# Dealing 384 weight rows over the DMA engines by another table

## Chip, cores and metric

The kernel runs on one core of a Trainium2 chip. The metric is the device time of one execution in microseconds, as the median of several executions. "Before" is the kernel given, "the changed kernel" is the one with the diff below. All verdicts use runs in the fast state; on this one core a slow run shows by its time alone: the 78.30 us run of before beside e1 has a granted clock of 0.835, where the fast runs of that job have 0.805 to 0.841. Ratios are the mean time of one kernel's fast runs over that of the other's in the same rounds, so they are not quite the ratio of the medians quoted beside them.

## The reference

One decode step of attention over a cached window, gated by a small MLP. Only the shapes matter here (shortened, not the full source):

```python
def reference(A_x, A_k_cache, A_v_cache, A_wq, A_wo, B_x, B_w1, B_b1, B_w2, B_b2):
    x = A_x                                   # (4, 1, 512), bf16
    xn = _layernorm(x)
    q = xn @ wq                               # wq 512 x 4096: 32 heads of 128
    k, v = last 1024 positions of the caches  # 8 kv heads, batch 4: 1 MB each a head
    o = softmax(q k^T * 128**-0.5) v
    s = o.reshape(4, 1, 4096) @ wo            # wo 4096 x 512: 4 MB
    g = silu(mlp(layernorm(xn)))              # w1 512 x 1792, w2 1792 x 512
    return x + s * g
```

Everything is read once, 28.85 MB. The time is nearly that of this stream: the DMA engines are 90% busy or more in 35 of 40 slices (below).

## The kernel before

The large loads are issued by SyncE (SP) in one long queue: wq, four K tiles, w1, the other four K tiles, four V tiles, w2, the other four V tiles, and then wo. The order of the last ones is what matters:

```python
    for n, (g0, g1) in enumerate(((0, 2), (2, 4), (4, 6), (6, 7))):
        load_wo(n, g0, g1, 0, 4)              # 1 MB, 1 MB, 1 MB, 0.5 MB
    d_w1st = pg.dma("sp", "w1st", lambda e: e.dma_start(
        wo_sb[:, 7, 0, :], A_wo[7 * 512:7 * 512 + 128, :]))      # 128 KB
```

The remaining 384 rows of wo (1 KB each) belong to the last head group. GpSimd loads them, in twelve calls, in the middle of the kernel:

```python
    R1 = (7 * 512 + 128) * D
    XS, b0 = [], 0
    for p0, n, r in ((0, 3, 5), (12, 2, 3), (20, 3, 1), (64, 2, 1), (72, 4, 5), (88, 2, 1)):
        XS.append((p0, n, r, b0))
        b0 += 4 * n * r
    XS = [(p0 + 32 * h, n, r, b + 192 * h) for h in range(2) for p0, n, r, b in XS]
    d_wox = [pg.dma("gp", "wox%d" % p0, lambda e, p0=p0, n=n, r=r, b=b: e.dma_start(
        wox_sb[p0:p0 + 4 * n, 0:r, :].rearrange("p j o -> p (j o)"),
        bass.AP(A_wo.tensor, R1 + b * D, [[r * D, n], [n * r * D, 4], [1, r * D]])), t_q)
        for p0, n, r, b in XS]
```

A call (p0, n, r) puts r rows into each of 4n partitions from p0 on. The first dimension of its source is n, and the table means it to run on the next n DMA engines, so that the six calls of a half take each of the 16 once. The packets of before fit this: q0 has 56 of 5120 bytes, 8 of 6144 and 14 of 4096, on 7 engines (3 + 4), 2 and 7 (3 + 2 + 2). The engine numbers below are names in this order; the label runs e1 and e2 test them. Each engine thus gets 4 partitions in each of the two halves: one row a partition is 8 KB an engine over both. The table is a hand-made dealing: engines 0 to 2 get 5 rows a partition, 3 and 4 get 3, 5 to 9 get 1, 10 to 13 get 5, and 14 and 15 get 1.

Because the rows then lie scattered over the partitions, GpSimd also builds 0/1 selector matrices, with which PE brings the attention output into the same order before it multiplies by the weights:

```python
    def rows_last():
        def fn(pe):
            for a in range(5):
                for j in range(3):
                    last = pe.matmul(psx[:, 160 + a * 4:164 + a * 4], selx[:, j, a, :],
                                     OTb[:, o + 4 + 4 * j:o + 8 + 4 * j], ...)
    ...
            wo([(wox_sb[:, a, :], OWx[:, a * 4:(a + 1) * 4], False, False) for a in range(5)],
               row_x, *d_wox)
```

The softmax here doesn't subtract the row's maximum and nothing guards it: scores larger than these inputs give would overflow.

Of the kernel before, what the change touches and what calls it, by code (L numbers as in the profile page):

```python
# [19 lines left out]
class _Program:  # L20
# [22 lines left out]
    def add(self, eng, fn, *deps, cls=None):  # L43
        op = _Op(eng, fn, deps, cls=cls)
        if eng == "pe":
            op.seg, op.once = self.seg, self.once
            if self.seg not in self.segs:
                self.segs.append(self.seg)
        self.ops[eng].append(op)
        return op  # L50
# [111 lines left out]
def bass_recurrent_scan__sliding_block_cached__mixer_channel_mlp__decode_kernel(  # L162
# [17 lines left out]
    BF16 = dt.bfloat16  # L180
    F32 = dt.float32

    B, D = 4, 512
# [22 lines left out]
    sb = nc.alloc_sbuf_tensor  # L206
# [4 lines left out]
    wq_sb = sb([128, 4, HQ * DH], BF16)  # L211
# [1 line left out]
    w1_sb = sb([128, 4, F], BF16)  # L213
    w2_sb = sb([128, FC, D], BF16)

    wox_sb = wq_sb[:, 0, 0:5 * D].rearrange("p (j o) -> p j o", j=5)
    kt_buf = sb([128, NKT, UT * 128], BF16)
    P_buf = sb([128, HKV, NC * 16], BF16)

# [33 lines left out]
    b2_sb = sb([4, 128], BF16)  # L253
    sel = sb([128, 4, 32], BF16)
    OW = sb([128, 4, 28], BF16)
    selx = sb([128, 3, 5, 128], BF16)
    OWx = sb([128, 20], BF16)
    hT = sb([128, FC, 32], BF16)

    OTb = sb([128, HKV * 16], BF16)  # L260
# [17 lines left out]
    add = pg.add  # L278
# [71 lines left out]
    a = add("act", lambda e: e.activation(sq1[:, :], vt1[:, :], AF.Sqrt), v)  # L350
# [9 lines left out]
    a = add("act", lambda e: e.activation(sq2[:, :], vt2[:, :], AF.Sqrt), v)  # L360
# [239 lines left out]

    R1 = (7 * 512 + 128) * D
    XS, b0 = [], 0
    for p0, n, r in ((0, 3, 5), (12, 2, 3), (20, 3, 1), (64, 2, 1), (72, 4, 5), (88, 2, 1)):
        XS.append((p0, n, r, b0))
        b0 += 4 * n * r
    XS = [(p0 + 32 * h, n, r, b + 192 * h) for h in range(2) for p0, n, r, b in XS]
# [13 lines left out]
    psx = psS[0]  # L620
# [16 lines left out]
    def rows_last():  # L637
        def fn(pe):
            last = None
            o = 7 * 16  # L640
            for a in range(5):
                for j in range(3):
                    last = pe.matmul(psx[:, 160 + a * 4:164 + a * 4], selx[:, j, a, :],
                                     OTb[:, o + 4 + 4 * j:o + 8 + 4 * j],
                                     start=(j == 0), stop=(j == 2))
            return last
        t = add("pe", fn, ep[HKV - 1], c_sx)
        return add("dve", lambda e: e.tensor_copy(OWx[:, :], psx[:, 160:180]), t)

    for g in range(HKV):  # L650
        pg.seg = ("v", g // NG)
# [31 lines left out]
    def wo(tiles, *deps):  # L683

        def fn(pe):
            last = None
            for w, o, st, sp in tiles:
                for c in range(4):
                    last = pe.matmul(psM[:, PS_W + c * 4:PS_W + (c + 1) * 4],  # L689
                                     w[:, c * 128:(c + 1) * 128], o,  # L690
                                     start=(st and c == 0), stop=sp, skip_group_check=True)
            return last
        return add("pe", fn, *deps)

    for g0, g1, i0, i1, d in d_wo:
        wo([(wo_sb[:, g, i, :], OW[:, i, g * 4:(g + 1) * 4], g == 0 and i == 0, False)
            for g in range(g0, g1) for i in range(i0, i1)], d, row_w, mlp["g"])
        if g0 == 0:
            row_x = rows_last()
            wo([(wox_sb[:, a, :], OWx[:, a * 4:(a + 1) * 4], False, False) for a in range(5)],  # L700
               row_x, *d_wox)
    t_w = wo([(wo_sb[:, 7, 0, :], OTb[:, 7 * 16:7 * 16 + 4], False, True)], d_w1st,
             ep[HKV - 1])
# [6 lines left out]
    t = add("pe", lambda pe: pe.transpose(psS[0][0:16, 0:128], sg_sb[:, :], ident32[:, :]),  # L710
            v, c_id32)
# [56 lines left out]
```

## Time and profile before

| what | value | from |
|---|---|---|
| time | 77.11 us (76.94 to 77.13, 3 runs) | timed runs |
| span of the profiled run | 75.0 us | page |
| DMA | 28.95 MB, mean 386 GB/s, 90% busy or more in 35 of 40 slices | page |
| busiest compute engine | PE, 67% of the span | page |
| end of the chain | fourth wo load lands at 71.52 us, then a tail | chain |

The way to read it: when the DMA line is full almost from end to end and every compute engine has room, look for what ends the transfers. In before's trace each wo load has 16 landing events; those of the fourth come between 69.77 and 71.52 us, and PE goes on at 71.57, after the last. So the balance between the engines counts (e4 tests it), and the page shows only their mean. Below, a "heavy" engine is one that gets 5 or 6 rows a partition from the table, and a "light" one gets 1.

### The profile page before, as it was taken

What the parts mean: (1) busy time and instruction counts of PE and PEld (TensorE: products, weight loads), DVE (VectorE), ACT (ScalarE), POOL (GpSimd) and SP (SyncE); (2) the same over time, 40 slices, a digit from 0 to 9 for tenths busy, and PEclk for the clock granted to TensorE, in tenths of its full rate; (3) what the DMA queues carried; (4) which work ended last, traced back from release to release, by engine and by line L of the source; (5) the groups of instructions that cost most, each with busy time, mean ns of one, the idle gap of its engine ahead of it and who ended that gap; (6) DMA issues with size and microseconds to landing.
All of it is one profiled execution on the core that took longest, in us unless ns stands there. A gap on an engine that the chain in (4) does not pass through costs nothing.

```text
span 75.0 us, 2371 instructions
## 1 busy us (share of the span) xinstructions
PE 50.3 (67%) x1043; PEld 40.5 (54%) x1043; DVE 40.6 (54%) x84; ACT 12.5 (17%) x21; POOL 17.8 (24%) x46
## 2 busy tenths in 40 slices
PE   0000650959999997297999959880669984686560
PEld 0000300259999996387999837650329753486430
DVE  0778200036999986097999904999800576430020
ACT  0611000090002304100311333841030000000000
POOL 6994000089999872000000000000000000000000
PEclk9999999999999999999999999995555555555555
DMA  1899999999999999999999999999999999999800
GB/s 28 262 419 422 456 419 411 428 424 428 414 456 429 410 395 422 410 425 428 428 424 428 419 424 457 435 420 400 424 428 419 428 421 408 424 419 419 314 4 2
DMA packets 4680, 28.95 MB, mean 386 GB/s; under 512 B 1007, under 2 KB 1139, under 8 KB 2114
## 3 DMA queue, kind: packets, MB, share of 16 engines
q1 hardware_dynamic: 4016, 28.45, 91.0%
q0 software_dynamic: 608, 0.40, 1.7%
q8 instruction: 5, 0.08, 0.4%
q10 hardware_dynamic: 50, 0.01, 0.1%
q14 instruction: 1, 0.01, 0.0%
HBM read 28.85 MB, written 0.00 MB: 384 GB/s over the span
## 4 chain that ended last, share of the span: by engine, by line
DMA 26%; PE 19%; DVE 3%; SPq 2%; ACT 2%; issue 1%
DMA wo_sb<-in_A_wo_dram 26%; PE psK L383 8%; PE psS L403 4%; PE psO L422 3%; SPq L674 2%; PE psK L514 1%; PE psM L689 1%; PE psS L399 1%; DVE kt_buf L524 1%; DVE den_sb L439 1%; ACT P_buf L411 1%; ACT kt_buf L523 1%; PE psS L429 1%; PE psS L710 1%; PE psK L518 0%
## 5 line engine op out<-in xcount | busy, mean ns | idle before, releaser
L389 DVE COPY kt_buf<-psK 128x1024 bf16<-128x1024 bf16 x32 | 20.9, 690 | 4.2 <-PE psK L383 4.2
L383 PE MATMUL psK<-ident,kv_buf 128*128 128x128 bf16 x256 | 19.9, 228 | 2.2 <-PEq L101 2.2
L383 PEld LDWEIGHTS psK<-ident,kv_buf 128*128 128x128 bf16 x256 | 16.0, 103 | 2.4 <-issue 1.8
L403 PE MATMUL psS<-qR,kt_buf 128*128 128x16 bf16 x256 | 10.5, 170 | 0.0
L403 PEld LDWEIGHTS psS<-qR,kt_buf 128*128 128x128 bf16 x256 | 9.6, 96 | 1.1
L422 PEld LDWEIGHTS psO<-P_buf,kv_buf 128*128 128x128 bf16 x256 | 7.5, 101 | 3.7 <-issue 2.0
L422 PE MATMUL psO<-P_buf,kv_buf 128*128 128x16 bf16 x256 | 7.9, 172 | 1.6 <-PEq L101 1.3
L607 POOL DMA_DIRECT2D wq_sb<-in_A_wo_dram x12 | 6.7, 604 | 8.5 <-PE psO L471 8.5
L411 ACT ACTIVATE P_buf<-psS 128x512 bf16<-128x512 f32 x8 | 4.8, 597 | 22.4 <-PE psS L403 22.4
L439 DVE TENSOR_REDUCE den_sb<-psS 128x16 f32<-128x512 f32 x8 | 5.5, 682 | 1.3 <-PE psS L429 1.2
L471 PE MATMUL psO<-wq_sb,xT 128*32 128x512 bf16 x32 | 3.8, 627 | 3.0 <-DMA wq_sb<-in_A_wq_dram 2.7
L455 PE MATMUL psS<-ident,xn_bf 4*128 4x4 bf16 x4 | 0.3, 172 | 7.8 <-DVE y_bf L362 7.8
L689 PE MATMUL psM<-OW,wo_sb 128*128 128x4 bf16 x112 | 3.6, 167 | 2.3 <-DMA wo_sb<-in_A_wo_dram 2.3
L689 PEld LDWEIGHTS psM<-OW,wo_sb 128*128 128x128 bf16 x112 | 3.3, 104 | 2.6 <-DMA wo_sb<-in_A_wo_dram 2.5
L455 PEld LDWEIGHTS psS<-ident,xn_bf 4*128 4x128 bf16 x4 | 0.2, 114 | 7.8 <-DVE y_bf L362 7.8
L477 DVE CAST q_sb<-psO 128x512 bf16<-128x512 f32 x1 | 0.7, 691 | 6.6 <-PE psO L471 6.6
L615 POOL TENSOR_SCALAR_AFFINE_SELECT selx<-ones_bf 128x8 bf16<-128x8 bf16 (+4 forms) x14 | 4.0, 282 | 1.0
L429 PE MATMUL psS<-P_buf,ones_bf 128*128 128x512 bf16 x8 | 3.9, 482 | 0.0
L548 PE MATMUL psK<-w_sb,hT 128*4 128x512 bf16 (+1 forms) x14 | 1.9, 622 | 2.9 <-DMA w_sb<-in_B_w_dram 2.9
L471 PEld LDWEIGHTS psO<-wq_sb,xT 128*32 128x32 bf16 x32 | 0.9, 128 | 5.1 <-DMA wq_sb<-in_A_wq_dram 3.7
L399 PE MATMUL psS<-negm,ind 128*128 128x512 bf16 x8 | 3.0, 379 | 0.0
L706 DVE TENSOR_TENSOR sg_sb<-psM,g_sb 128x16 f32<-128x16 f32 x1 | 0.2, 184 | 5.2 <-PE psM L689 5.2
(80 smaller groups left out, 43.7 us busy)
## 6 DMA issues: line engine op xcount, KB each, us to landing
kv_buf<-in_A_k_cache_dram SPq DMA_DIRECT2D x8, 1024.0 KB, 12.5
kv_buf<-in_A_v_cache_dram SPq DMA_DIRECT2D x8, 1024.0 KB, 12.4
wq_sb<-in_A_wq_dram SPq DMA_DIRECT2D x2, 2048.0 KB, 9.6
w_sb<-in_B_w_dram SPq DMA_DIRECT2D x2, 1792.0 KB, 22.5
wo_sb<-in_A_wo_dram SPq DMA_DIRECT2D x3, 1024.0 KB, 16.5
wo_sb<-in_A_wo_dram SPq DMA_DIRECT2D x1, 512.0 KB, 19.2
wq_sb<-in_A_wo_dram POOLq DMA_DIRECT2D x2, 80.0 KB, 11.9
wo_sb<-in_A_wo_dram SPq DMA_DIRECT2D x1, 128.0 KB, 17.5
```

The source lines that it names most:

```text
L383: last = pe.transpose(psK[n % NB][:, j * 128:(j + 1) * 128], kv_buf[:, lg, u * UT + j, :], ident[:, :])
L389: cp[r, n] = bank[n % NB] = add("dve", lambda e: e.tensor_copy(kt_buf[:, n % NKT, :], psK[n % NB][:, 0:1024]), t, kt_user[n % NKT], cls="cp")
L399: pe.matmul(psS[lg % 2][:, 0:512], ind[:, :], negm[:, :], start=True, stop=False, skip_group_check=True)
L403: last = pe.matmul(psS[lg % 2][:, c * 16:(c + 1) * 16], kt_buf[:, n % NKT, j * 128:(j + 1) * 128], qR[:, lg * 16:(lg + 1) * 16], start=Fal ...
L411: ex[g] = add("act", lambda e: e.activation(P_buf[:, g, :], psS[lg % 2][:, 0:512], AF.Exp, scale=SCALE), sc[r, n], cls="ex")
L422: last = pe.matmul(pso[:, 0:16], kv_buf[:, NG + lg, c, :], P_buf[:, lg, c * 16:(c + 1) * 16], start=(c == 0), stop=(c == NC - 1))
L429: den[g] = add("pe", lambda pe: pe.matmul(psS[g % 2][:, 0:512], ones_bf[:, :], P_buf[:, lg, :], start=True, stop=True))
L439: v = add("dve", lambda e: e.tensor_reduce(den_sb[:, cs], bass.AP(psS[g % 2], 0, [[512, 128], [1, 16], [16, NC]]), AX.X, ALU.add), den[g])
L471: last = pe.matmul(psO[m // 4][32 * s:32 * s + 32, 0:512], xT[:, c, :], wq_sb[:, c, m * 512:(m + 1) * 512], start=(c == 0), stop=(c == 3), ...
L607: d_wox = [pg.dma("gp", "wox%d" % p0, lambda e, p0=p0, n=n, r=r, b=b: e.dma_start(wox_sb[p0:p0 + 4 * n, 0:r, :].rearrange("p j o -> p (j o)"),
L615: c_sx = add("gp", lambda e, p0=p0, n=n, r=r, b=b, j=j: e.affine_select(selx[:, j, 0:r, p0:p0 + 4 * n], ones_bf[:, 0:4 * n * r], [[1, r], ...
L689: last = pe.matmul(psM[:, PS_W + c * 4:PS_W + (c + 1) * 4], w[:, c * 128:(c + 1) * 128], o, start=(st and c == 0), stop=sp, skip_group_che ...
```

## The change

The intent is to move rows from engines that finish late to engines that finish early. Engines 0 to 2 and 11 to 13 get 6 rows a partition instead of 5, engines 3 and 4 get 2 instead of 3, and engine 10 gets 1 instead of 5. The total stays at 384 rows in twelve calls. Six row slots in place of five make PE's part a little longer.

```diff
-    wox_sb = wq_sb[:, 0, 0:5 * D].rearrange("p (j o) -> p j o", j=5)
+    wox_sb = wq_sb[:, 0, 0:6 * D].rearrange("p (j o) -> p j o", j=6)
...
-    selx = sb([128, 3, 5, 128], BF16)
-    OWx = sb([128, 20], BF16)
+    selx = sb([128, 3, 6, 128], BF16)
+    OWx = sb([128, 24], BF16)
...
-    for p0, n, r in ((0, 3, 5), (12, 2, 3), (20, 3, 1), (64, 2, 1), (72, 4, 5), (88, 2, 1)):
+    for p0, n, r in ((0, 3, 6), (12, 2, 2), (20, 3, 1), (64, 3, 1), (76, 3, 6), (88, 2, 1)):
...
-            for a in range(5):
+            for a in range(6):
...
-        return add("dve", lambda e: e.tensor_copy(OWx[:, :], psx[:, 160:180]), t)
+        return add("dve", lambda e: e.tensor_copy(OWx[:, :], psx[:, 160:184]), t)
...
-            wo([(wox_sb[:, a, :], OWx[:, a * 4:(a + 1) * 4], False, False) for a in range(5)],
+            wo([(wox_sb[:, a, :], OWx[:, a * 4:(a + 1) * 4], False, False) for a in range(6)],
```

## The prediction

What the first rival would cost, and its chance of one in six, which moved the point to 77.05 and the range up to 77.45, were estimates; measured are the two parts of the delay, 0.9 us for a fetch and 0.5 us on the packet behind it. That a load waits for its last engine is shown by the 16 landing events above.

> **What bounds the kernel now.** I read four views, in this order: the page's slices and queues, the chain that ended last, the busy time by stretch near the end, and the timeline of the same stretch. The page first:

> ```profile
> DMA  1899999999999999999999999999999999999800
> ...
> q1 hardware_dynamic: 4016, 28.45, 91.0%
> q0 software_dynamic: 608, 0.40, 1.7%
> q8 instruction: 5, 0.08, 0.4%
> ...
> q14 instruction: 1, 0.01, 0.0%
> ```

> The DMA engines are full from slice 2 to slice 37 of 40, so the 28.95 MB stream sets the length and no compute engine does. The twelve GpSimd loads are q0: 0.40 MB, 1.7% of the engines' time. They load rows 128 to 511 of the last head's output weights, 384 rows of 1 KB, dealt unevenly over the DMA engines. The chain confirms which load ends it:

> ```profile
> 52.35 19.17 DMA wo_sb<-in_A_wo_dram
> 71.52 0.05 issue
> 71.57 0.70 PE psM L689 x20
> ...
> 72.30 0.20 DVE sg_sb L706
> ...
> 72.54 0.40 PE psS L710
> ...
> 72.96 0.28 DVE o_bf L712
> ```

> Here the fourth output-weight load lands at 71.52, and a fixed tail follows: 20 matmuls, a multiply, a transpose, an add and the store. A load has landed only when its slowest DMA engine is done, so what counts is the last engine, not the mean. The stretches (length, then busy time and count of each engine, then granted clock, DMA share, GB/s) show that the engines don't end together:

> ```profile
> 63.00:69.70 6.70, 4.88 (x148) 4.10 (x148) 1.82 (x7) 0.00 (x0) 0.00 (x0) 0.50 1.02 420
> 69.70:70.30 0.60, 0.00 (x0) 0.00 (x0) 0.00 (x0) 0.00 (x0) 0.00 (x0) 0.50 0.90 362
> 70.30:70.90 0.60, 0.56 (x21) 0.56 (x21) 0.00 (x0) 0.00 (x0) 0.00 (x0) 0.50 0.71 280
> 70.90:71.60 0.70, 0.49 (x19) 0.41 (x16) 0.00 (x0) 0.00 (x0) 0.00 (x0) 0.50 0.40 135
> ```

> The share falls in the last 1.9 us: some engines are idle. To see which, I went to the trace's single DMA packets. They don't name their engine, but within an engine each packet starts 3 to 4 ns before the end of the last, so they can be chained into 16 rows that fit from 1.8 us to the end. The sizes of a row's q0 packets then tell its rows a partition (eight of 5120 bytes for 5 rows, four of 6144 for 3, two of 4096 for 1), and its number of 256-byte ACT packets narrows the engine. The last packet of the last weight load ends, in us: engines 0 to 2 at 71.18, 71.06, 70.98; engines 3 and 4 at 71.56 and 70.23; engines 5 to 7 at 71.30, 71.23, 70.01; engines 8 and 9 at 71.42 and 69.77; engines 10 to 13 at 71.24, 71.05, 71.04, 71.17; engines 14 and 15 at 71.25 and 69.90 (the order within a group is not sure). The mean is 70.90 and the last 71.56. Perfect dealing could thus gain 0.66 us of 77.11, 0.9%. That is the most that any change of this kind can win, and it decides the chances.

> The four early engines are the light ones that got no instruction fetch. Every light engine that ends late carries one 16384-byte q8 packet (at 23.35, 30.34, 48.34, 57.26), and engine 3, the last of all, the 8192-byte q14 packet at 42.06. A fetch takes about 0.9 us itself and the packet behind it about 0.5 us longer (at 48.34: 878 ns, then 1082 in place of 535). So the light dealing on engines 5 to 9, 14 and 15 pays where a fetch falls, and wastes where none does.

> [...]

> **The change, part by part.** The number of GpSimd calls (12), the bytes (393 KB) and every other load stay. The dealing moves. One packet costs its duration less the overlap: 196 - 3 = 193 ns for 5120 bytes, 231 for 6144, 155 for 4096. Engines 0 to 2 and 11 to 13: eight packets of 6144 for eight of 5120, 8 x 38 = +0.30 us. Engines 3 and 4: 2 rows instead of 3; if two partitions still share a packet, four of 4096 for four of 6144, 4 x 76 = -0.30. Engine 10: two of 4096 for eight of 5120, 310 - 1544 = -1.23. Sum: 6 x 0.304 - 2 x 0.304 - 1.234 = about 0, as it must be. Adding these to the ends: engines 0 to 2 at 71.48, 71.36, 71.28; 3 and 4 at 71.26 and 69.93; 10 at about 70.01 (I take it as the one of 71.24, whose GpSimd packets come early like those of the lower engines; 69.82 otherwise); 11 to 13 at 71.36, 71.34, 71.48; the rest unchanged, with 71.42 their last. The new last is 71.48 against 71.56: -0.08 us. If engine 10 is the one of 71.05, the one of 71.24 goes to 71.55 and the gain is 0.01. The worst engine is relieved, but six others are pushed into its place; and the 1.2 us taken from engine 10 make it a fifth idle one.

> PE gets 3 more selector matmuls and 4 more weight matmuls. They lie here:

> ```profile
> 66.29 0.56 PE L643 MATMUL psS<-OTb,selx 128*128 128x4 bf16 x15
> ...
> 67.13 0.69 PE L689 MATMUL psM<-OWx,wq_sb 128*128 128x4 bf16 x20 [0.27 <-DVE OWx L648]
> ...
> 67.85 1.01 PE L689 MATMUL psM<-OW,wo_sb 128*128 128x4 bf16 x32
> ...
> 70.34 1.02 PE L689 MATMUL psM<-OW,wo_sb 128*128 128x4 bf16 x32 [1.48 <-DMA wo_sb<-in_A_wo_dram]
> ```

> 3 x 0.56/15 + 4 x 0.69/20 = 0.25 us, in front of a wait of 1.48 us for the third weight load: hidden. On GpSimd the memset of 1.79 us grows by 2304/1920 to 2.15 and four affine selects of 0.28 us go; all that ends near 29 us and is read at 66.29: hidden. The tail is the same. Sum: -0.08 us, 77.03.

> **The rivals.** First, an instruction fetch falls on a heavier engine. The fifth fetch starts at 71.05, on an engine idle by then, or (it fits to 3 ns) right behind the last packet of the engine of 71.05, one of 10 and 11. [...] On engine 11 it would then lie in front of the last packets and cost 0.6 to 1.2 us: 77.7 to 78.3. For it: the exact fit, and that the engine isn't known. Against it: five other engines are idle then, the fetches so far went to 5 to 9, 14 and 15, and the change makes engine 10 light, as if for such a fetch. I give it one in six. Second, fetches wander between executions; then the dealing is a lottery before and after. Against it: the 0.19 us spread of the three times before, where one fetch on a heavy engine would cost over 1 us. It would give 77.0 to 78.4. Third, the real gain: if the fetch engines differ from my chaining and engine 10 was late in most runs, up to 0.5 us is won, 76.6. The trace has engine 10 no later than its neighbours, so this is weak.

> **Range and chances.** Without a collision, 77.03 with the run-to-run 0.1 us: 76.85 to 77.2. The collision draws the upper end out, so the point is 77.05 and the range 76.8 to 77.45. Perfect balance is worth 0.9%, so a gain over 2% is almost excluded (1%). A loss over 2% (1.5 us) needs two mishaps at once or a stall that I don't see (3%). Within 2%: 96%.

> **What would show it.** In the changed profile q0 should carry 0.40 MB in fewer large packets: 48 of 6144 bytes, and 24 of 4096 (8 on engines 3 and 4, 16 on the eight light engines). The chain should still end on the fourth weight load, landing at 71.4 to 71.5; five early engines instead of four, so the DMA share between 70.3 and 70.9 should fall from 0.71 to about 0.66; and PE's third weight group should still wait over 1 us. It is wrong if the load lands after 71.9 (look for a q8 packet before 71 us in a heavy row) or before 71.2.

## The result, and the profile after

The changed kernel takes 77.06 us (77.00 to 77.13, 4 runs), before in the same rounds 77.04 us (76.94 to 77.13, 4 runs). The ratio is 1.0003, 95% interval 0.9985 to 1.0021: the same. Executions over 1.5% slower than the fastest of the same kernel are left out of the means. All eight runs are fast.

The DMA lines of the changed kernel's page:

```profile
DMA  2899999999999999999999999999999999999800
...
q1 hardware_dynamic: 4016, 28.45, 91.1%
q0 software_dynamic: 608, 0.40, 1.7%
q8 instruction: 5, 0.08, 0.4%
...
q14 instruction: 1, 0.01, 0.0%
```

The stream is the same in packets, bytes and time. The end of the chain of waits, with start and length in us:

```profile
53.58 17.96 DMA wo_sb<-in_A_wo_dram
71.54 0.05 issue
71.58 0.70 PE psM L689 x20
...
72.31 0.20 DVE sg_sb L706
```

The fourth wo load lands at 71.54 us, where it landed at 71.52 before, and the tail is the same. The load was issued later (53.58 against 52.35), which made no difference here: it landed 0.02 us later, and in both kernels the DMA engines were full before it (share 1.02 from 63.0 to 69.7 us). The last stretches of the changed kernel (columns as in the prediction: length, then busy time and count of PE, PEld, DVE, ACT and POOL, the granted clock, DMA share, GB/s):

```profile
69.70:70.30 0.60, 0.00 (x0) 0.00 (x0) 0.00 (x0) 0.00 (x0) 0.00 (x0) 0.50 1.00 386
70.30:70.90 0.60, 0.56 (x21) 0.56 (x22) 0.00 (x0) 0.00 (x0) 0.00 (x0) 0.50 0.67 275
70.90:71.60 0.70, 0.47 (x19) 0.39 (x16) 0.00 (x0) 0.00 (x0) 0.00 (x0) 0.50 0.44 157
```

More of the stream falls into the very last stretch (157 GB/s against 135), less into the one before (275 against 280): more engines are busy to the end, and more are idle before it. PE's part, from the timeline:

```profile
66.29 0.64 PE L643 MATMUL psS<-OTb,selx 128*128 128x4 bf16 x18
...
67.21 0.80 PE L689 MATMUL psM<-OWx,wq_sb 128*128 128x4 bf16 x24 [0.28 <-DVE OWx L648]
...
70.34 1.01 PE L689 MATMUL psM<-OW,wo_sb 128*128 128x4 bf16 x32 [1.47 <-DMA wo_sb<-in_A_wo_dram]
```

PE's addition is 0.64 - 0.56 + 0.80 - 0.69 = 0.19 us, and the wait for the third load is still 1.47 us long.

The single packets, chained into 16 rows as in the prediction, show where the ends went. (Such a row is the string of packets of one DMA engine, not a weight row.) The numbers are the end of each row's last weight packet in us; a star marks a row with an instruction fetch or the 8 KB q14 packet before that end:

```
                  before                              changed
engines 0-2       71.18 71.06 70.98                   71.56 71.43 71.47
engines 3, 4      71.56* 70.23                        71.25* 70.34
light engines     71.30* 71.23* 71.42* 71.25*         71.24* 71.17* 71.22* 71.47*
                  70.01 69.77 69.90                   69.85 69.93 70.10, engine 10: 70.00
engines 10/11-13  71.24 71.05 71.04 71.17             71.50 71.51 71.38
mean, last        70.90, 71.56                        70.96, 71.56
```

Engine 3 was relieved and six heavy engines moved to its place; one of engines 0 to 2 now ends last. The last end is 71.56 us in both.

What a fetch (a 16384-byte packet of q8, the queue that the page calls "instruction") costs its row can be read in both traces. The four before 69 us take 0.88 to 0.99 us, where a stream packet of that size takes 0.61, and the stream packet right behind each takes 0.47 to 0.55 us longer than others of its size (847 ns for 309 after the one at 30.34 us). That is about 1.4 us in all, and in before it is the difference between fetched and spared light engines (71.2 to 71.4 against 69.8 to 70.0). PE itself keeps working through before's fetches at 23.35, 48.34 and 57.26 us.

### The profile page after: what moved, and what is told of

The parts are those of the page before. It is cut to its first block, busy times and chain, and to the rows that moved or that the text cites. A ratio compares the mean times of both kernels' runs of the same rounds, so it can differ in the third digit from the quotient of the medians.

```text
span 75.1 us, 2385 instructions
## 1 busy us (share of the span) xinstructions
PE 52.5 (70%) x1050; PEld 42.5 (57%) x1050; DVE 40.7 (54%) x84; ACT 12.5 (17%) x21; POOL 18.2 (24%) x46
## 2 busy tenths in 40 slices
DMA packets 4680, 28.95 MB, mean 386 GB/s; under 512 B 1013, under 2 KB 1145, under 8 KB 2114
## 3 DMA queue, kind: packets, MB, share of 16 engines
q1 hardware_dynamic: 4016, 28.45, 91.1%
## 4 chain that ended last, share of the span: by engine, by line
DMA 24%; PE 24%; DVE 3%; SPq 2%; ACT 2%; issue 1%
DMA wo_sb<-in_A_wo_dram 24%; PE psK L383 12%; PE psS L403 4%; PE psO L422 2%; SPq L674 2%; PE psS L399 1%; PE psK L514 1%; PE psM L689 1%; DVE den_sb L439 1%; DVE kt_buf L524 1%; ACT P_buf L411 1%; ACT kt_buf L523 1%; PE psS L429 1%; PE psS L710 1%; PE psK L518 0%
## 5 line engine op out<-in xcount | busy, mean ns | idle before, releaser
L383 PE MATMUL psK<-ident,kv_buf 128*128 128x128 bf16 x256 | 22.0, 244 | 1.2 <-PEq L101 1.2
L383 PEld LDWEIGHTS psK<-ident,kv_buf 128*128 128x128 bf16 x256 | 17.9, 111 | 1.3 <-issue 1.3
L689 PE MATMUL psM<-OW,wo_sb 128*128 128x4 bf16 x112 | 3.6, 167 | 2.3 <-DMA wo_sb<-in_A_wo_dram 2.3
L689 PEld LDWEIGHTS psM<-OW,wo_sb 128*128 128x128 bf16 x112 | 3.3, 104 | 2.5 <-DMA wo_sb<-in_A_wo_dram 2.5
L615 POOL TENSOR_SCALAR_AFFINE_SELECT selx<-ones_bf 128x72 bf16<-128x72 bf16 (+3 forms) x14 | 4.1, 294 | 1.0
L706 DVE TENSOR_TENSOR sg_sb<-psM,g_sb 128x16 f32<-128x16 f32 x1 | 0.2, 185 | 5.2 <-PE psM L689 5.2
```

Source lines behind the costliest of these rows:

```text
L383: last = pe.transpose(psK[n % NB][:, j * 128:(j + 1) * 128], kv_buf[:, lg, u * UT + j, :], ident[:, :])
L615: c_sx = add("gp", lambda e, p0=p0, n=n, r=r, b=b, j=j: e.affine_select(selx[:, j, 0:r, p0:p0 + 4 * n], ones_bf[:, 0:4 * n * r], [[1, r], ...
L689: last = pe.matmul(psM[:, PS_W + c * 4:PS_W + (c + 1) * 4], w[:, c * 128:(c + 1) * 128], o, start=(st and c == 0), stop=sp, skip_group_che ...
```

## The experiments

Which engine is which had been guessed in part, so the first two runs name them. The others test whether the last engine sets the end at all, against the rival that the total number of bytes does and the dealing is irrelevant; both predict "the same" for this change. All twelve kernels gave correct results. Each job compares with before on its own chip.

**Labels on the engines (e1, e2).** Seven tiny loads on the ACT queue, which nobody reads, mark the engines by how many of them each carries:

```diff
+    d_lab = [pg.dma("act", "lab%d" % k, lambda e, i=i, k=k: e.dma_start(
+        lab[0:k, i, :], x_r[0:k, :])) for i, k in enumerate((2, 6, 7, 9, 11, 13, 15))]
```

> The kernel before with seven tiny extra loads on the ACT queue, of 2, 6, 7, 9, 11, 13 and 15 rows, which nobody reads. If a load of k rows goes to engines 0 to k-1, each chained row of packets gets a number of 256-byte packets that names its engine. All theories expect the same time within 0.2 us. The last engine should be engine 3 near 71.56 us, as before; I expect engine 10 to be the row with the fifth 16 KB fetch, and the four early rows to be 4, one of 5 to 7, 9, and 14.

> The changed kernel with the same seven label loads. Engines 0 to 2 and 11 to 13 should end last, at 71.4 to 71.6 us; five engines should end near 70 us: 4, 10 and one each of 5 to 7, of 8 and 9, and of 14 and 15. If fetches go to fixed engines, the fetched engines are the same as in the labelled kernel before; if they wander, they differ.

**PE's addition alone (e3).** The dealing of before with six slots:

```diff
-    selx = sb([128, 3, 5, 128], BF16)
+    selx = sb([128, 3, 6, 128], BF16)
     ... and the other lines with 5 or 20, but not the table
```

> The dealing of before, with the sixth row slot of the change: 3 more selector matmuls and 4 more weight matmuls (times zero), the larger memset and output copy. Theory (the last DMA engine sets the end, PE's addition hides in the wait for the third weight load): 0.0 us, at most 0.1. Rival (the change gained something that PE's addition took back): 0.2 us slower, 77.25.

Measured: 76.93 us (76.85 to 77.07, 6 runs) against 77.00, ratio 0.9997 (0.9984 to 1.0011). PE's addition costs nothing, so it hides no gain.

**Four rows more on two engines (e4).**

```diff
-    for p0, n, r in (..., (64, 2, 1), (72, 4, 5), (88, 2, 1)):
+    for p0, n, r in (..., (64, 2, 5), (72, 4, 3), (88, 2, 1)):
```

> Before with engines 8 and 9 at 5 rows a partition instead of 1 and 10 to 13 at 3 instead of 5; same bytes, same calls. Theory (the last engine sets the end): the fetched engine of 8 and 9 goes from 71.42 to 72.63, 1.07 us behind the 71.56 of before: 78.1 us, +1.4%. Rival (the stream is bound by its total bytes, the dealing doesn't matter): 77.04 unchanged.

Measured: 78.04 us (77.86 to 78.19, 4 runs) against 77.00, ratio 1.0137 (1.0118 to 1.0157). That is less than 2%, but the interval lies clear of 1. The bytes are the same, and the time grows by 1.05 us where 1.07 was worked out. Its end of the chain, and its last stretch:

```profile
52.64 19.98 DMA wo_sb<-in_A_wo_dram
72.63 0.05 issue
```

```profile
71.60:72.80 1.20, 0.97 (x36) 0.89 (x34) 0.00 (x0) 0.00 (x0) 0.00 (x0) 0.50 0.05 20
```

A DMA share of 0.05 is about one engine of 16 (1/16 is 0.06). One engine alone works for the last microsecond and the whole kernel waits for it. The rival falls: dealing counts, one to one, by the last engine.

**Other dealings, laid out one after the other (e5 to e8).** These put the rows of successive calls into successive partitions, so that any grouping fits:

```diff
-    for p0, n, r in ((0, 3, 5), (12, 2, 3), ...):
-        XS.append((p0, n, r, b0))
+    for n, r in CALLS:
+        XS.append((p0, n, r, b0))
+        p0, b0 = p0 + 4 * n * (r > 0), b0 + 4 * n * r
```

> The change's largest part alone: engine 10 goes from 5 rows a partition to 1, and its rows go to engines 7 and 8 (1 to 3), which the labelled runs showed idle for the last 1.3 us. 14 calls. Theory: no engine that ends late is touched but engine 10, which ended 0.5 us before the last: 0.0 us (76.9 to 77.1). Rival (engine 10 with its fetch held up the end in most runs): 0.2 to 0.5 us faster.

> The change's relief without its push: engine 10 at 1 row, engines 3 and 4 at 2, and the freed rows on the idle engines 7 and 8 (4 rows) in place of engines 0 to 2 and 11 to 13, which stay at 5. Theory: engine 3 falls to 71.1 us and the fetched engines 5, 6, 9 and 14 at about 71.3 become the last; 0.1 us faster than before (76.9) and than the changed kernel. Rival (dealing is irrelevant below some level): unchanged.

> 3 rows a partition on every engine, four calls of 8 engines. Theory: the fetched engines 5, 6, 9 and 14 get 2 rows more, 0.61 us, and become the last at about 72.05 us: 0.5 us slower, 77.5 (+0.65%). Rival (total bytes bind): unchanged.

> No rows on the fetched engines 5, 6, 9 and 14 [...], and over both halves 9 partition-rows on engines 0 to 2 and 10 to 13, 10 on 7 and 8, 4 on 3 and 4, 5 on 15. Theory: all but 15 end between 70.9 and 71.3 us, where before the last is 71.5: 0.25 us faster, 76.75 (-0.3%). [...]

Measured: 79.20, 79.30, 78.19 and 80.61 us, ratios 1.0165, 1.0181, 1.0014 and 1.0316. Before on this chip was 78.05 us, nine of its eleven runs between 77.99 and 78.34 and two at 77.00 and 77.11. All four expectations failed, and one thing stands out that the dealing does not explain: in all four the stream packets are longer than 309 ns for 5 to 15 us in the middle, on many engines. These runs decide nothing about the rows. Two things were suspected, the disturbed chip and the new layout.

**The layout alone (e9).** The dealing and the calls of before, in the layout of e5 to e8.

> The dealing and the twelve calls of before, but the rows laid one group after the other over partitions 0 to 127, as in the last four runs[...]. Theory [...]: 1 us or more slower than before, with stream packets longer than 309 ns between 20 and 40 us. Rival (those runs were slow because that chip was disturbed): unchanged against before of the same job.

Measured, on a chip where before took 77.07 us: 78.79 us (78.59 to 79.14, 4 runs), ratio 1.0231 (1.0206 to 1.0256), slower. The stretch around the second group of calls, first of before, then of this run:

```profile
24.00:32.00 8.00, 6.26 (x149) 5.88 (x147) 5.19 (x10) 1.79 (x3) 3.80 (x14) 1.00 1.01 415
32.00:40.00 8.00, 7.55 (x167) 7.07 (x164) 7.45 (x12) 1.19 (x2) 0.00 (x0) 1.00 1.01 426
```

```profile
24.00:32.00 8.00, 5.24 (x130) 4.83 (x126) 4.83 (x9) 1.79 (x3) 3.88 (x14) 1.00 0.99 324
32.00:40.00 8.00, 6.79 (x117) 6.58 (x118) 5.30 (x8) 0.60 (x1) 0.00 (x0) 0.79 1.01 423
```

The DMA engines are just as busy but move 324 GB/s instead of 415: (415 - 324) x 8 = 728 KB short, which is 1.7 us at 424 GB/s, the whole loss. Outside this stretch the rate is that of before: 432 GB/s from 15 to 24 us (before 425), 423 from 32 to 40 (426) and 425 from 40 to 63 (424). The two kernels deal the same rows in the same calls and differ in the partitions that are written, so the placement costs 1.7 us. Why it does is not shown. So the layout can account for the losses of e5 and e6 (1.3 and 1.4 us) and for part of that of e8 (2.5 us), whose remainder is unexplained; what these runs would have told about the dealing stays open.

**Uniform dealing in before's placement (e10).** Four calls of 8 engines, 3 rows each, at partitions 0, 64, 32 and 96, so that each engine's rows lie in the 8 partitions that before's table gives it.

> 3 rows a partition on every engine, four calls of 8[...]. Theory: the fetched engines 5, 6, 9 and 14 become the last at about 72.05 us, 0.5 us slower than before: 77.5 on an undisturbed chip. Rival (total bytes bind, dealing is irrelevant): unchanged.

Measured: 77.14 us (77.00 to 77.25 in the fast runs, and one of 78.34) against 77.07, ratio 1.0010 (0.9995 to 1.0025). I expected 77.5. In its trace the fetched rows do end last, at 71.62 to 71.84 us, and the others at 70.15 to 70.53 (engine 3, with the q14 packet, at 71.14); the last fetched one is some 0.2 us earlier than the sum said. The likely reason is in q0: with four calls each row carries 8 small packets (4 to 8 bytes), with twelve 30 to 37 (4 to 16 bytes; 530 in the 16 rows of before). At some 6 ns each (9 ns less the overlap of 3, in before) that is, by estimate, about 0.15 us for every engine. Besides, the time outside the profiled span was 77.12 - 75.3 = 1.8 us here and 77.07 - 75.0 = 2.1 us before. The tuned table thus gains 0.28 us at the last engine (71.84 against 71.56, one trace each) over no tuning at all, and by this reading its eight extra calls cost nearly as much. No run changes the number of calls alone at uniform dealing.

**The dealing by named engines (e11).** Nothing on the fetched engines, in 18 calls, some meant for a single engine and some of a few bytes, meant only to pass an engine over.

> The dealing by named engines [...]: nothing on the fetched engines 5, 6, 9 and 14; over both halves 8 partition-rows on 0 to 2, 3 on 3 and 4, 10 on 7, 8 and 15, 9 on 10 to 13; 18 calls, six more than before. Theory: the last engine at 71.1 to 71.3 us instead of 71.5, 0.2 to 0.3 us faster than before (76.75). If the calls of one engine do not go to one engine, it is slower by 0.5 us or more.

Measured: 80.93 us against 77.07, ratio 1.0508. Its packets are stretched from 25 to 39 us as in e9. My guess was that the calls meant for one engine, or the tiny ones, did not go where they should; no run shows it. The dealing that would beat both kernels was not reached this way.

**Six calls (e12).** The dealing and the partitions of before, both halves in one call each:

```diff
-    for p0, n, r in ((0, 3, 5), (12, 2, 3), (20, 3, 1), (64, 2, 1), (72, 4, 5), (88, 2, 1)):
+    for p0, n, r in ((0, 3, 10), (12, 2, 6), (20, 3, 2), (64, 2, 2), (72, 4, 10), (88, 2, 2)):
...
-    XS = [(p0 + 32 * h, n, r, b + 192 * h) for h in range(2) for p0, n, r, b in XS]
```

> The dealing of before, [...] but both halves in one: six GpSimd calls of twice the rows (10, 6, 2, 2, 10, 2 a partition, 64 partitions) instead of twelve. PE gets 15 more selector and 20 more weight matmuls, some 1.3 us, just inside the 1.48 us wait for the third weight load. Theory from the uniform run (a GpSimd call costs every DMA engine some small packets, about 20 ns, and each call some 30 ns outside the profiled span): 0.3 us faster than before, 76.75 (-0.4%). Rival (calls cost nothing, the uniform run was just lucky in its start): unchanged; and if PE's addition does not fit in its wait, 0.2 us or more slower.

(Its 20 and 30 ns a call are estimates from e10: 22 to 29 small packets fewer at some 6 ns, and 2.07 - 1.82 = 0.25 us less outside the span, each over eight calls.)

Measured: 76.74 us median, but in two groups: 76.54, 76.59, 76.68, 76.81 and 77.68, 77.79. Before: 76.98 (76.82 to 77.17, 11 runs). The ratio of 0.9981 (0.9941 to 1.0022) mixes the two, since 77.68 counted as fast. Four of six runs show the 0.3 us that fewer calls were to bring; over all fast runs the gain is not shown. The profiled run is the one of 77.68, and it shows what the other group is:

```profile
71.35 0.59 PE L689 MATMUL psM<-OW,wo_sb 128*128 128x4 bf16 x16 [0.23 <-DMA wo_sb<-in_A_wo_dram]
72.89 0.19 PEld L689 LDWEIGHTS psM<-OTb,wo_sb 128*128 128x128 bf16 x4 [1.03 <-DMA wo_sb<-in_A_wo_dram]
72.89 0.27 PE L689 MATMUL psM<-OTb,wo_sb 128*128 128x4 bf16 x4 [0.95 <-DMA wo_sb<-in_A_wo_dram]
```

PE waits another microsecond for the very last load, of 128 KB. In the packets, on the row of the fifth instruction fetch, that fetch came between the last data packet and the 4-byte packet behind it. I call that one the report: in before q1 has 416 of them, 16 for each of the 26 SP loads, as many as landing events, and the last one of the 128 KB load starts at 71.55 us, 0.31 us before the load's last landing event (71.86).

```
row of the fifth fetch, start and end in ns, bytes
before:     ... 71002-71048 1024 | 71044-71053 4 (report) | 71050-71982 16384 (fetch)
changed:    ... 69945-69991 1024 | 69987-69996 4 (report) | 69993-70925 16384 (fetch)
six calls:  ... 70793-70839 1024 | 70836-71765 16384 (fetch) | 71751-71776 4 (report)
```

In the first two the report went out first. In the six-call run it went out 0.92 us later, and landed at 72.85 us, 1.10 us after it started; the others of that load land 0.3 us after. Why it took so long to land is not shown. The two together make 2.0 us.

This may be the slow group of before too. By an estimate from these numbers: its report on engine 10 starts at 71.04; 2.0 us later is 73.06, where PE is ready for that load at 71.99. The loss would be 1.07 us, and 77.04 + 1.07 = 78.1; the slow runs of before are 77.99 to 78.34. None of those was profiled, so this is an inference. In the changed kernel, by the same estimate, the accident would land at 69.99 + 2.0 = 72.0 us, just when PE is ready (72.03), and would cost nothing. Relieving engine 10 may thus guard against the slow group. That is not shown: the changed kernel was timed only four times, on a chip where before had no slow run, and the one slow run of the uniform kernel (78.34) does not fit this account, since its engine 10 also ends early.

## Why the prediction was right, point by point

- **The last DMA engine sets the end.** Right, and shown by e4: same bytes, one engine late, 1.05 us measured for 1.07 worked out.
- **At most 0.66 us to win, so within 2%.** The change did stay within 2%. No run tests the bound itself; no other dealing beat before, and even no dealing at all (e10) is only 0.1% from it.
- **The packet arithmetic.** The changed kernel's q0 has 48 packets of 6144 bytes and 24 of 4096, as foreseen, so two partitions do share a packet on engines 3 and 4.
- **-0.08 us by engine.** The direction was right for every group but not for engine 4, and the sizes were off. The six heavy rows were to end at 71.28 to 71.48 and end at 71.38 to 71.56; engine 4 was to end at 69.93 and ends at 70.34; the load landed at 71.54, not 71.4 to 71.5. The step that failed is the one that added the change to the ends of one trace as if those were fixed. They are not: the first stream packets start between 1.8 and 2.6 us and those begun before 4 us are lengthened by up to 1.1 us in all, differently on each engine and in each run. Start and lengthening (what the 16384-byte packets begun before 4 us took beyond 609 ns each) add up to between 2.50 and 2.96 us over the 16 rows of before, mean 2.75, and to between 2.55 and 2.93 us, mean 2.78, in the changed kernel. Engine 4 alone had 0.41 us more of it than before, against the 0.30 us of rows it was spared: 0.41 - 0.30 = 0.11, and it ended 0.11 us later. This term is several times the predicted gain of 0.08 us, so that the total came out right (77.06 for 77.05) says little about the sum by engine.
- **Engine 10.** I took it as the row ending at 71.24. The label run shows it as the row with the fifth fetch (70.98 there, so the one of 71.05 in the first trace). It mattered little: the heaviest of 11 to 13 went to 71.51, between the two figures that I gave for the two cases (71.48 and 71.55).
- **PE hides.** Right (e3: ratio 0.9997). The addition was 0.19 us rather than 0.25.
- **GpSimd hides.** Right, but I said that four affine selects go; there are 14 before and after, and I had misread repeat counts. The memset grew to 2.13 us as worked out; all ends at 29.1 us, 37 us before it is read.
- **DMA share 0.66 between 70.3 and 70.9.** 0.67 was measured, but partly by accident: the fifth fetch sat on an otherwise idle engine through that stretch, 0.6 us of 9.6 engine-microseconds, 0.06. Without it the share would be 0.61.
- **The fetch rival.** It did not happen in the changed kernel's profile: the fetch came a full microsecond sooner than before (69.99), but right behind the last packet of engine 10, which was light by then. The prediction had it 0.2 us sooner "or more", for a reason that no run shows; in before, in the changed kernel and in e1 and e2 it starts within 4 ns of the end of its row's report. How close this is to an accident e12 shows.
- **Wandering fetches.** Not seen: in both labelled runs the fetches fell on the same engines (9 and 10 untold apart in the second).

## What to carry to other kernels

When a stream over 16 DMA engines bounds a kernel, the landing of its last load is the maximum over the engines (in e4 72.63 us, after a last microsecond with a DMA share of 0.05); work out the end of each engine, and compare a planned gain with the scatter of those ends between runs before tuning a table. The partitions that small loads write beside such a stream can matter: the same rows and calls in others cost 1.7 us (e9), so time the placement by itself. That the loads should also be few is suggested by e10 and four runs of e12, but not shown. Where a tail waits for the last load, look in the packets whether an instruction fetch got in front of its completion report; one profiled run (e12) shows this, with a report 0.92 us late that took 1.10 us to land instead of 0.3. That a spare engine prevents it is not tested.
